# Block-sparse attention with a gated feed-forward: three split products for half of chunk 0's down-projection, and a later start of chunk 1's attention

## The chip, the cores and the metric

One core of a Trainium2 chip runs the whole program. The metric is the device time in microseconds (us), the median of several runs. The engines are TensorE (PE in the profile; PEld is its weight load), VectorE (DVE), ScalarE (ACT), GpSimd (POOL) and SyncE (SP). SyncE and GpSimd serve here mainly as queues that issue DMAs.

## The reference

```python
mask = |blk_i - blk_j| <= 1  or  an edge block (0 or 23) in row or column
mask |= the 3 sampled key blocks of the query's block
attn = softmax(where(mask, q @ k.T / 8, -1e9))       # 4 batches, 8 heads, 768 x 64, blocks of 32
x = (attn @ v) as [3072 tokens, 512]
h = x @ w_in                                          # 512 -> 2048
out = (h * sigmoid(1.702 * h)) @ w_out                # 2048 -> 512
```

Everything is float32. The two weight matrices reach the kernel as 64-bit words and are turned into float32 on the chip.

## The kernel before

**Chunks and steps.** The 3072 tokens are cut into 6 chunks of 512. A chunk's feed-forward is 16 steps, one for each block f of 128 of the 2048 inner columns. Step m (`tick`, L644) has f = m mod 16. In it TensorE makes 12 products for the up-projection of block f (`up`, L492: four slices of 128 inputs, three products each), and then the down-projection of the step before (`down`, L534), which adds to four PSUM banks. ScalarE and VectorE make the gate between them (`gate`, L506): a tanh from PSUM, and g = (tanh + 1) * h. In steps 0 to 12 ScalarE first copies h out of its one PSUM bank (L514), so the next step's up-projection can have that bank once the copy is done.

**Split products.** TensorE takes float32 operands either plainly (one product is then two instructions) or in a reduced form, `float32r`, one instruction. A value is split into a high part (a cast by ScalarE) and a low part (value minus high part, by VectorE); high x high, high x low and low x high add up to the product. Every up-projection does that. The down-projection does it from chunk 1 on: L562 and L563 take ghi with the two parts of the weight, L558 takes glo with the high part. `gate_hi` (L519) casts g to ghi behind the first half of the down-projection, `gate_lo` (L526) makes glo at the start of the next step, and the weight's parts lie in a ring of three tiles `wout`, which `split` (L486) fills from `wst`, read back from DRAM (`stream`, L480). In chunk 0 the down-projection is plain: four products a step, two in each half (L546), from g and the float32 weight `whole[f]`.

**Unpacking the weights.** During chunk 0 the generator `weights` (L407) turns the 64-bit words into float32, block by block, in the order w_in 0, w_in 1, w_out 0, w_in 2, w_out 1, and so on. For each block GpSimd's queue fetches 512 KB (L426, five blocks ahead); ScalarE makes a first pass over the high words into a tile `a` (L438); VectorE does three integer operations on it (L449, L456, L463). For w_in, ScalarE then casts the high part (L467) and VectorE makes the low part while the next block is under way (L453). `a` is one of two tiles in rotation. For w_out the first pass writes a tile of the `ghi` or `glo` ring instead, where the finished weight stays as `whole[f]`, and SyncE's queue copies it to DRAM (L470, `ws`), from where chunks 1 to 5 read it. The first pass over w_out block f waits in the generator until at most four blocks are ahead of the down-projection (L459). Each `yield` ends a piece; a step runs 8 pieces if an attention unit begins in it, else 9: none or two at its start, four between tanh and g, four or three at its end (L649).

**The attention.** A chunk's tokens are 8 units. Chunk 0's attention runs before step 0; chunk 1's is put between the steps of chunk 0 by `plan` (L605), in quarters of a step: a unit's scores at its starting quarter, its transposes four quarters later, and its values where the next unit's scores stand. The 8 units share quarters 4 to 56 evenly (starts 4, 10, 17, 23, 30, 36, 43, 49). Behind each starting quarter `loads` (L223) issues the keys that a freed buffer can take: on SyncE's queue four transfers and six more whose address comes from a register, each waiting until TensorE is through with the buffer.

**Order.** The program order is written out by hand; each engine and each queue works through its own instructions strictly in it, and waits where a tile is not ready or not yet free.

Of the kernel before, what the change touches and what calls it, by code (L numbers as in the profile page):

```python
# [9 lines left out]
F32 = mybir.dt.float32  # L10
F32R = mybir.dt.float32r
I32 = mybir.dt.int32
AF = mybir.ActivationFunctionType
ALU = mybir.AluOpType
# [4 lines left out]
P = 128  # L19
# [5 lines left out]
DM = H * D  # L25
DF = 2048
NCT = DM // P
NF = DF // P
# [7 lines left out]
WRING = 3  # L36
LAG = 1
QT = 4
BIG = float(2 ** 33)
SCALE = 1.0 / float(D) ** 0.5  # L40
REBASE = 2.0 ** -112
AHEAD = 5


class Kernel:
# [361 lines left out]
    def weights(self):  # L407

        nc = self.nc
        todo = []  # L410
        for f in range(NF + LAG):
            if f < NF:
                todo.append((f, 0))
            if f >= LAG:
                todo.append((f - LAG, 1))
        self.ready = set()
        tiles = {}

        def fetch(k):
            if k < len(todo):  # L420
                f, i = todo[k]
                if i == 0:
                    raw = self.const.tile([P, 2 * DM], I32, name=f"win{f}")
                else:
                    raw = self.work.tile([P, 2 * DM], I32, name="raw", bufs=3)
                nc.gpsimd.dma_start(out=raw, in_=self.w64[i][f])  # L426
                tiles[k] = {"raw": raw.rearrange("p (a b) -> p a b", b=2)}

        def first(k):


            f, i = todo[k]
            if i == 0:
                a = self.work.tile([P, DM], I32, name="a")
            else:
                a = self.work.tile([P, DM], F32R, name=("ghi", "glo")[f % 2]).bitcast(I32)
            tiles[k]["a"] = a
            nc.scalar.activation(out=a.bitcast(F32), in_=tiles[k]["raw"][:, :, 1].bitcast(F32), func=AF.Abs, scale=REBASE)  # L438

        for k in range(AHEAD):  # L440
            fetch(k)
        yield
        first(0)
        yield
        for k, (f, i) in enumerate(todo):
            fetch(k + AHEAD)
            raw, a = tiles[k]["raw"], tiles[k]["a"]
            low, high = raw[:, :, 0], raw[:, :, 1]
            nc.vector.tensor_scalar(out=a, in0=a, scalar1=3, scalar2=None, op0=ALU.logical_shift_left)  # L449
            yield  # L450
            if k > 0 and todo[k - 1][1] == 0:
                t, w = self.win[todo[k - 1][0]], tiles[k - 1]["a"].bitcast(F32)
                nc.vector.tensor_tensor(out=t[:, DM:2 * DM], in0=w, in1=t[:, 0:DM].bitcast(F32), op=ALU.subtract)  # L453
                self.ready.add(todo[k - 1])
                yield
            nc.vector.scalar_tensor_tensor(out=a, in0=high, scalar=-0x80000000, in1=a, op0=ALU.bitwise_and,  # L456
                                           op1=ALU.bitwise_or)
            if k + 1 < len(todo):
                while todo[k + 1][1] == 1 and (not self.turned or todo[k + 1][0] - 4 > self.downs - 1):  # L459
                    yield  # L460
                first(k + 1)
            yield
            nc.vector.scalar_tensor_tensor(out=a, in0=low, scalar=29, in1=a, op0=ALU.logical_shift_right,  # L463
                                           op1=ALU.bitwise_or)
            if i == 0:
                self.win[f] = self.const.tile([P, 2 * DM], F32R, name=f"win{f}")
                nc.scalar.copy(out=self.win[f][:, 0:DM], in_=a.bitcast(F32))  # L467
            else:
                self.whole[f] = a.bitcast(F32)
                nc.sync.dma_start(out=self.ws[f], in_=self.whole[f])  # L470
                self.ready.add((f, i))
            yield

    def need(self, f, i):
        while (f, i) not in self.ready:
            next(self.conv, None)
# [40 lines left out]
        self.g[m] = [g]  # L517

    def gate_hi(self, m):  # L519
        if m < NF:  # L520
            return
        ghi = self.work.tile([P, CT], F32R, name="ghi")
        self.nc.scalar.copy(out=ghi, in_=self.g[m][0])  # L523
        self.g[m].append(ghi)
# [9 lines left out]
    def down(self, m, part):  # L534
        nc = self.nc
        if m < 0:
            return
        c, f = divmod(m, NF)
        if c == 0:
            self.need(f, 1)  # L540
        o = [self.bank[3 + n] for n in range(NN)]
        tk = [slice(n * P, (n + 1) * P) for n in range(NN)]
        last = f == NF - 1
        if c == 0:
            for n in range(2 * part, 2 * part + 2):
                nc.tensor.matmul(o[n], self.g[m][0][:, tk[n]], self.whole[f], start=(f == 0), stop=last)  # L546
            if part == 1:
                del self.g[m]
                self.downs = m + 1
                if last:  # L550
                    self.store(c, o)
            return
        _, ghi, glo = self.g[m]
        w = self.wout[m % WRING]
        woh, wol = w[:, 0:DM], w[:, DM:2 * DM]

        def low(n):
            nc.tensor.matmul(o[n], glo[:, tk[n]], woh, start=False, stop=last)  # L558

        if part == 0:  # L560
            for n in self.order(c):
                nc.tensor.matmul(o[n], ghi[:, tk[n]], woh, start=(f == 0), stop=False)  # L562
                nc.tensor.matmul(o[n], ghi[:, tk[n]], wol, start=False, stop=False)  # L563
                if last:
                    low(n)
            return
        if not last:
            for n in range(NN):
                low(n)
        del self.g[m]  # L570
        self.downs = m + 1
        if last:
            self.store(c, o)
# [31 lines left out]
    def plan(self):  # L605

        chunks = [[g for g in self.items if g["unit"]["n"] // CU == c] for c in range(NC)]
        at, starts = {}, []
        for c in range(1, NC):
            begin = 4 if c == 1 else 4 * QT * (4 * c - 4) - 8  # L610
            end = 4 * QT * 4 * c - 8
            dense = sum(not self.sparse(g) for g in chunks[c])
            room, count = end - begin - 4 * dense, len(chunks[c]) - dense
            for k, g in enumerate(chunks[c]):
                q = room + 4 * (k - count)
                if self.sparse(g):
                    q = min(8 * k, room - 6 * (count - k)) if room >= 7 * count else room * k // count
                starts.append((begin + q, g))
        starts.append((end, None))
        put = lambda q, part, g: at.setdefault(q, []).append((part, g))  # L620
        for k, (q, g) in enumerate(starts):
            before = starts[k - 1][1] if k else None
            turn = q + 4
            if g is not None:
                if q >= 0:
                    put(q, self.scores, g)
                turn = q + (4 if self.sparse(g) else 2)
                put(turn, self.transposes, g)
            if before is not None:
                assert q >= 0  # L630
                put(q, self.values, before)
                if before["end"]:
                    put(turn, self.turn, before)
        return at
# [49 lines left out]
    def first(self):  # L684
# [19 lines left out]
        for p in range(CU // 2):  # L704
# [20 lines left out]
            if final:  # L725
                weights(1)
            finish(behind)
            behind = self.transposes(b)
            if final:
                self.turned = True  # L730
                weights(2)
            finish(behind)
            if final:
                weights(1)
# [76 lines left out]
```

## Time and profile before

| | |
|---|---|
| median of 3 runs | 782.81 us (782.76 to 785.66) |
| profiled execution | 784.16 us, span 782.5 us |
| TensorE busy | 749.5 us (96% of the span) |
| VectorE busy | 395.5 us (51%) |
| ScalarE busy | 364.8 us (47%) |
| chain of waits | TensorE 92%, DMA 5% |

The span is what the trace covers; the profiled execution's own time is 1.7 us longer. A busy TensorE is one whose matmul records leave no gap. The shares are averages: chunk 0, from about 61 to 204 us, has other proportions than the rest, since the weights are unpacked there. In the timelines below a duration is that of one instruction; instructions of one engine overlap a little, so the time that one costs its engine is the distance between two starts.

### The profile page before, as it was taken

The numbers are of one execution on the slowest core, as the hardware profiler recorded it, in microseconds if no ns is written. First come the engines' busy times: TensorE is split into PE (matmuls) and PEld (weight loads), VectorE is DVE, ScalarE is ACT, GpSimd is POOL, SyncE is SP. The second block draws the span as 40 slices with busy tenths as digits, with TensorE's granted clock in tenths as the row PEclk, the third lists the DMA queues.
The fourth block names the chain that finished last, engine by engine and source line by source line (L and its number), as shares of the span: only waits on it lengthen the run. The fifth ranks groups of instructions, "written<-read, shape, count | busy, mean of one in ns | idle before, by whom it ended". The sixth has DMA issues, their size and how long they took to land.

```text
span 782.5 us, 19089 instructions
## 1 busy us (share of the span) xinstructions
PE 749.5 (96%) x7520; PEld 559.9 (72%) x7520; DVE 395.5 (51%) x1044; ACT 364.8 (47%) x919; POOL 68.4 (9%) x109
## 2 busy tenths in 40 slices
PE   3778999999999999999999999999999999999997
PEld 2554666666777777777777777777777777888885
DVE  4367888863554354445445544444554444443333
ACT  3374575643555444444444544444545444333232
POOL 3342122100000001000000000000000000000000
PEclk9899999999999999999999999999999999999999
DMA  8989988764744437564444455435574231141111
GB/s 247 326 295 345 314 286 310 239 203 142 219 146 144 125 107 226 164 175 136 150 122 141 144 175 147 145 116 154 162 234 156 82 108 29 40 107 42 54 41 54
DMA packets 62235, 128.20 MB, mean 164 GB/s; under 512 B 7713, under 2 KB 27938, under 8 KB 61634
## 3 DMA queue, kind: packets, MB, share of 16 engines
q1 hardware_dynamic: 49954, 85.09, 36.0%
q0 software_dynamic: 11376, 41.03, 15.6%
q8 instruction: 59, 0.97, 0.5%
q10 hardware_dynamic: 816, 0.86, 0.4%
q14 instruction: 30, 0.25, 0.1%
HBM read 116.47 MB, written 10.49 MB: 162 GB/s over the span
## 4 chain that ended last, share of the span: by engine, by line
PE 92%; DMA 5%; SPq 1%; issue 1%; DVE 0%; POOL 0%; ACT 0%; POOLq 0%; DVEq 0%
PE bank L501 13%; PE bank L503 11%; PE bank L502 11%; PE bank L562 10%; PE bank L558 10%; PE bank L563 10%; PE bank L546 7%; PE bank L314 6%; PE bank L340 5%; PE bank L263 5%; DMA kg<-in_kb_dram 2%; PE bank L348 2%; PE bank L275 2%; DMA vmid<-in_v_dram 1%; PE bank L393 1%; DMA vown<-in_v_dram,vidx 1%
## 5 line engine op out<-in xcount | busy, mean ns | idle before, releaser
L501 PE MATMUL bank<-xhi,win 128*128 128x512 f32 x384 | 164.4, 428 | 0.6 <-ACT xhi L400 0.5
L516 DVE SCALAR_TENSOR_TENSOR g<-g,bank 128x512 f32<-128x512 f32 x83 | 57.0, 687 | 190.8 <-ACT g L509 190.8
L503 PE MATMUL bank<-xhi,win 128*128 128x512 f32 x384 | 152.1, 396 | 0.4 <-DVE win L453 0.4
L502 PE MATMUL bank<-xlo,win 128*128 128x512 f32 x384 | 151.9, 396 | 0.0
L298 ACT ACTIVATE ex<-bank,nm 128x256 f32<-128x256 f32 (+1 forms) x176 | 84.7, 491 | 130.0 <-DVE nm L286 130.0
L509 ACT ACTIVATE g<-bank 128x512 f32<-128x512 f32 x96 | 57.5, 598 | 158.9 <-PE bank L503 158.9
L562 PE MATMUL bank<-wout,ghi 128*128 128x512 f32 x320 | 128.6, 402 | 0.0
L563 PE MATMUL bank<-wout,ghi 128*128 128x512 f32 x320 | 126.3, 395 | 0.0
L490 DVE TENSOR_TENSOR wout<-wst,wout 128x512 fp32r<-128x512 f32 x80 | 55.4, 692 | 78.3 <-ACT wout L489 77.3
L558 PE MATMUL bank<-wout,glo 128*128 128x512 f32 x320 | 90.1, 395 | 0.0
L501 PEld LDWEIGHTS bank<-xhi,win 128*128 128x128 f32 x384 | 72.5, 189 | 21.6 <-issue 2.7
L286 DVE CUSTOM_DVE_ANT_1 bank<-bank,bias 128x256 f32<-128x256 f32 x176 | 73.7, 441 | 24.8 <-PE bank L263 20.3
L503 PEld LDWEIGHTS bank<-xhi,win 128*128 128x128 f32 x384 | 72.4, 189 | 18.7 <-DVE win L453 0.7
L502 PEld LDWEIGHTS bank<-xlo,win 128*128 128x128 f32 x384 | 72.6, 189 | 16.5 <-issue 2.6
L219 POOL DMA_INDIRECT vown<-in_v_dram,vidx x44 | 43.1, 980 | 409.9 <-PE bank L340 292.5
L523 ACT CAST ghi<-g 128x512 fp32r<-128x512 f32 x80 | 49.7, 621 | 45.5 <-DVE g L516 45.5
L558 PEld LDWEIGHTS bank<-wout,glo 128*128 128x128 f32 x320 | 60.1, 188 | 14.7
L319 ACT COPY pt<-bank 128x512 f32<-128x512 f32 (+1 forms) x112 | 56.9, 560 | 29.0 <-PE bank L314 28.9
L562 PEld LDWEIGHTS bank<-wout,ghi 128*128 128x128 f32 x320 | 60.2, 188 | 13.8
L563 PEld LDWEIGHTS bank<-wout,ghi 128*128 128x128 f32 x320 | 60.2, 188 | 13.5
L263 PE MATMUL bank<-kg,qt 64*32 64x256 f32 x1408 | 52.0, 399 | 15.3 <-DMA kg<-in_kb_dram 13.2
L531 DVE TENSOR_TENSOR glo<-g,ghi 128x512 fp32r<-128x512 f32 x80 | 54.7, 684 | 0.7 <-ACT ghi L523 0.7
(101 smaller groups left out, 890.1 us busy)
## 6 DMA issues: line engine op xcount, KB each, us to landing
wst<-ws SPq DMA_DIRECT2D x80, 256.0 KB
kg<-in_kb_dram SPq DMA_DIRECT2D x142, 128.0 KB
kg<-in_kb_dram SPq DMA_DIRECT2D x22, 384.0 KB
win<-in_moe_w_in_dram POOLq DMA_DIRECT2D x16, 512.0 KB, 8.3
raw<-in_moe_w_out_dram POOLq DMA_DIRECT2D x16, 512.0 KB, 4.3
kg<-in_kT_dram SPq DMA_DIRECT2D x4, 1536.0 KB
vown<-in_vd_dram SPq DMA_DIRECT2D x8, 768.0 KB
qt<-in_q_dram SPq DMA_DIRECT2D x22, 256.0 KB
```

The source lines that it names most:

```text
L263: nc.tensor.matmul(sps[h][BLK * c:BLK * (c + 1), n * i:n * (i + 1)].rearrange("p (n s) -> p n s", s=BLK), self.qt[r][rows, bi, UT * pair + ...
L286: nc.vector.tensor_tensor_reduce(out=at, in0=at, in1=bias, scale=-SCALE, scalar=3.0e38, op0=ALU.add, op1=ALU.min, accum_out=un["nm"][:, ha ...
L298: nc.scalar.activation(out=ex, in_=sps[h][:, n * k:n * (k + 1)], func=AF.Exp, bias=un["nm"][:, half, c:c + 1], scale=-1.0, accum_out=un["r ...
L319: copies.append(lambda pt=pt, ps=ps, m=m: nc.scalar.copy(out=pt[:, 0:m], in_=ps[:, 0:m]))
L501: nc.tensor.matmul(h, wih[:, k], hi[:, k], start=(k == 0), stop=False)
L502: nc.tensor.matmul(h, wih[:, k], lo[:, k], start=False, stop=False)
L503: nc.tensor.matmul(h, wil[:, k], hi[:, k], start=False, stop=(k == NCT - 1))
L509: nc.scalar.activation(out=g, in_=self.h, func=AF.Tanh, scale=0.851)
L516: nc.vector.scalar_tensor_tensor(out=g, in0=g, scalar=1.0, in1=h, op0=ALU.add, op1=ALU.mult)
L558: nc.tensor.matmul(o[n], glo[:, tk[n]], woh, start=False, stop=last)
L562: nc.tensor.matmul(o[n], ghi[:, tk[n]], woh, start=(f == 0), stop=False)
L563: nc.tensor.matmul(o[n], ghi[:, tk[n]], wol, start=False, stop=False)
```

## The change

In chunk 0 the down-projection of blocks 8 to 15 takes the split form of the later chunks; blocks 0 to 7 stay plain. For it the unpacked w_out block f (f of 8 and more) lies in a tile `a`, is copied to DRAM from there, and is split at once into the ring `wout` (ScalarE's cast, and VectorE's low part in `rest`). The first pass over such a block waits until at most three blocks are ahead (the length of that ring). `gate_hi` and `gate_lo` work from step 8 on. Chunk 1's units share quarters 8 to 56 instead of 4 to 56 (starts 8, 14, 20, 26, 32, 38, 44, 50). Chunk 0's sums are stored by the code that the later chunks use.

```diff
+NFULL = 8
...
-            if i == 0:
+            if i == 0 or f >= NFULL:
                 a = self.work.tile([P, DM], I32, name="a")
             else:
                 a = self.work.tile([P, DM], F32R, name=("ghi", "glo")[f % 2]).bitcast(I32)
...
+        def rest(k):
+            t, w = tiles[k]["to"], tiles[k]["a"].bitcast(F32)
+            nc.vector.tensor_tensor(out=t[:, DM:2 * DM], in0=w, in1=t[:, 0:DM].bitcast(F32), op=ALU.subtract)
+            self.ready.add(todo[k])
...
-            if k > 0 and todo[k - 1][1] == 0:
-                t, w = self.win[todo[k - 1][0]], tiles[k - 1]["a"].bitcast(F32)
-                nc.vector.tensor_tensor(out=t[:, DM:2 * DM], in0=w, in1=t[:, 0:DM].bitcast(F32), op=ALU.subtract)
-                self.ready.add(todo[k - 1])
+            if k > 0 and "to" in tiles[k - 1]:
+                rest(k - 1)
                 yield
...
-                while todo[k + 1][1] == 1 and (not self.turned or todo[k + 1][0] - 4 > self.downs - 1):
+                while todo[k + 1][1] == 1 and (not self.turned or todo[k + 1][0] - (4 if todo[k + 1][0] < NFULL else WRING) > self.downs - 1):
                     yield
                 first(k + 1)
...
             if i == 0:
-                self.win[f] = self.const.tile([P, 2 * DM], F32R, name=f"win{f}")
-                nc.scalar.copy(out=self.win[f][:, 0:DM], in_=a.bitcast(F32))
+                self.win[f] = tiles[k]["to"] = self.const.tile([P, 2 * DM], F32R, name=f"win{f}")
+            elif f >= NFULL:
+                nc.sync.dma_start(out=self.ws[f], in_=a.bitcast(F32))
+                tiles[k]["to"] = self.wout[f % WRING]
+            if "to" in tiles[k]:
+                nc.scalar.copy(out=tiles[k]["to"][:, 0:DM], in_=a.bitcast(F32))
             else:
...
+        rest(len(todo) - 1)
+        yield
...
     def gate_hi(self, m):
-        if m < NF:
+        if m < NFULL:
             return
...
-        if c == 0:
+        if m < NFULL:
             for n in range(2 * part, 2 * part + 2):
                 nc.tensor.matmul(o[n], self.g[m][0][:, tk[n]], self.whole[f], start=(f == 0), stop=last)
             if part == 1:
                 del self.g[m]
                 self.downs = m + 1
-                if last:
-                    self.store(c, o)
             return
...
-            begin = 4 if c == 1 else 4 * QT * (4 * c - 4) - 8
+            begin = 8 if c == 1 else 4 * QT * (4 * c - 4) - 8
```

## Rows read from the trace of the kernel before

**Rows 1.** The page's chain that ended last, shares by engine.

```profile
PE 92%; DMA 5%; SPq 1%; issue 1%; DVE 0%; POOL 0%; ACT 0%; POOLq 0%; DVEq 0%
```

**Rows 2.** Stretches: length, busy time of each engine, PEclk, DMA share, GB/s.

```profile
60.00:78.00 18.00, 14.68 (x76) 8.85 (x77) 14.19 (x31) 8.40 (x20) 4.15 (x6) 0.91 0.97 341
78.00:130.00 52.00, 52.00 (x545) 33.02 (x544) 43.52 (x106) 31.99 (x78) 11.94 (x18) 1.00 0.91 302
130.00:160.00 30.00, 30.00 (x293) 18.85 (x291) 25.52 (x61) 18.89 (x45) 5.83 (x8) 1.00 0.79 259
```

**Rows 3.** The chain in order of time, 60 to 260 us: start, duration, what.

```profile
70.19 0.43 PE bank L502
...
73.58 3.43 PE bank L546 x8
...
77.02 0.87 PE bank L314 x8
...
80.70 1.02 PE bank L263 x32
...
81.73 1.03 PE bank L340 x64
...
176.13 1.02 PE bank L263 x32
...
209.53 0.93 PE bank L558 x4
```

**Rows 4.** TensorE's timeline, end of step 0 and step 1: start, duration, instruction.

```profile
64.58 0.39 PE L503 MATMUL bank<-xhi,win 128*128 128x512 f32 x1
66.99 0.62 PE L263 MATMUL bank<-kg,qt 64*32 64x256 f32 x4 [2.02 <-DMA vmid<-in_v_dram]
67.94 1.53 PE L263 MATMUL bank<-kg,qt 64*32 64x256 f32 x28 [0.33 <-DMA kg<-in_kb_dram]
```

**Rows 5.** ScalarE's timeline in step 0.

```profile
65.50 0.58 ACT L514 COPY wst<-bank 128x512 f32<-128x512 f32 x1
65.97 0.68 ACT L438 ACTIVATE a<-win 128x512 f32<-128x512 f32 x1
```

**Rows 6.** SyncE's queue, a load of keys and the copy behind it.

```profile
137.19 0.38 SPq L190 DMA_DIRECT2D qt<-in_q_dram  x1
...
145.76 0.44 SPq L470 DMA_DIRECT2D ws<-glo  x1
```

**Rows 7.** VectorE's timeline in steps 10 and 11.

```profile
150.79 0.43 DVE L286 CUSTOM_DVE_ANT_1 bank<-bank,bias 128x256 f32<-128x256 f32 x1
...
152.56 0.14 DVE L286 DVE_READ_ACCUMULATOR2_ANT nm<- 128x1 f32 x1
152.90 0.68 DVE L463 SCALAR_TENSOR_TENSOR ghi<-raw,ghi 128x512 int32<-128x512 int32 x1
153.50 0.42 DVE L449 TENSOR_SCALAR a<-a 128x512 int32<-128x512 int32 x1
153.95 0.69 DVE L456 SCALAR_TENSOR_TENSOR a<-win,a 128x512 int32<-128x512 int32 x1
154.68 0.69 DVE L463 SCALAR_TENSOR_TENSOR a<-win,a 128x512 int32<-128x512 int32 x1
...
159.39 0.68 DVE L516 SCALAR_TENSOR_TENSOR g<-g,wst 128x512 f32<-128x512 f32 x1
159.99 0.16 DVE L369 TENSOR_SCALAR rg<-rs 128x4 f32<-128x4 f32 x1
...
160.59 0.68 DVE L463 SCALAR_TENSOR_TENSOR a<-win,a 128x512 int32<-128x512 int32 x1
```

**Rows 8.** Groups by line and shape: busy, mean ns, idle before, releaser.

```profile
L453 DVE TENSOR_TENSOR win<-a,win 128x512 fp32r<-128x512 f32 x16 | 11.1, 691 | 6.6 <-ACT win L467 6.5
```

**Rows 9.** The page's DMA issues: count, KB each, median us to landing.

```profile
win<-in_moe_w_in_dram POOLq DMA_DIRECT2D x16, 512.0 KB, 8.3
raw<-in_moe_w_out_dram POOLq DMA_DIRECT2D x16, 512.0 KB, 4.3
```

## The prediction

> **What bounds the kernel now.** I read the page first: TensorE holds 92% of the chain of waits that ended last [rows 1]. So the reader should see that a microsecond is won only by issuing less on TensorE or by closing one of its few gaps, and lost wherever another engine makes it wait. Second, the table of stretches [rows 2]: inside the part that the change touches (steps 0 to 15, about 61 to 204 us) TensorE has no idle time after 78 us, its clock is full from there (2.4 GHz), and VectorE is the next engine, busy for 43.5 of 52 us and then for 25.5 of 30 us until the weights are unpacked. The DMA engines are 0.97 and 0.91 busy early, 0.79 by 130 to 160 us. So TensorE is the bound, with VectorE a tenth to a sixth behind it, and the early stretch has one gap. Third, the timelines of the engines, for what stands in whose queue.
>
> **The products.** A plain float32 product of 128x512 is issued as two instructions; eight of them advance the chain by 3.43 us, so one product costs 0.857 us. Four split products advance it by 0.93 us, 0.233 each, three of them 0.70 [rows 3]. Eight steps with four products each: 32 x (0.857 - 0.70) = 5.1 us less, all of it on the bound: **-5.1**. The weight loads lie under the products already.
>
> **The moved start.** In step 1 TensorE issues its last product of step 0 at 64.58, then waits 2.02 us and 0.33 us for the first unit's loads; behind it the clock falls (28 score products take 1.53 us where 32 take 1.02, and the next six products come 0.43 apart) [rows 3, 4]. Up to the transposes at 77.02 that is 12.2 us after the product that ends near 64.8, for 1.02 + 12 x 0.233 + 3.43 = 7.25 us of work at full clock. With the unit a step later, step 1's up-projection goes next. What is late then is its single PSUM bank: ScalarE reads step 0's sums until 65.50 + 0.58 = 66.1 [rows 5], 1.3 us of waiting. The scores come at about 72 us; in the trace their data was there at 67.9. Gain 12.2 - 7.25 - 1.3 = 3.7: **-3.7**. If the clock falls all the same, the gain is 1.8 less (0.6 on the scores, six products at 0.43 instead of 0.233), so 1.9; without the bank's wait 5.0. The loads that the units' scores trigger move with them, from steps 2, 5, 9 and 12 to 3, 6, 9 and 12; units now start every 6 quarters. The load of the first moved unit was issued before step 0 and stays.
>
> **Edits at nothing.** ScalarE gets a cast of g and a cast of the weight in each of eight steps, 0.62 us each; it is busy for 18.9 of 30 us in 130 to 160 us [rows 2], which hides them unless it stands still (below). The sums of chunk 0 are stored from the end of step 16 as before. The DMA bytes are the same.
>
> **The new wait.** From weight block 8 on, the unpacked down-projection weight lies in tile *a*, of which there are two, instead of *ghi/glo*. Its copy to DRAM is issued by SyncE, and ScalarE's first pass over block f+1 (L438) writes the same *a*, so it must wait until the copy of block f has landed. By the generator's yields the copy of block 10 is asked for in step 9 and the pass over block 11 stands at that step's end. Between them, in SyncE's order, stands a load of keys: its first transfer waits for the scores of the unit in quarter 38. One such load holds the queue from 137.19 to 145.76, 8.6 us, with a copy issued only behind it [rows 6]. Queued behind the waiting ScalarE pass are the cast of win, the copies of transposed weights and the next tanh; on VectorE L449 waits for the pass, and behind L449 stands the split of g (L531), which TensorE needs at the end of the next down-projection.
>
> The copy's landing has no row. The nearest are the weight fetches of 512 KB from the same engines: median 4.3 us and 8.3 us [rows 9]; half of 4.3 for half the bytes, 2.2 us, is my lower end, 8.3 the upper. I take 4.3, since the copy and that fetch are issued at the same point of the program. From the end of the scores: 8.6 + 4.3 + 0.6 (the pass, 0.68 busy, where the next instruction starts before its end [rows 5]) + 0.45 (L449) + 0.60 (the split) = 14.5 us until g's low part is there. TensorE meanwhile has values 1.03, down 12 x 0.233, up 2.8, eight transposes 0.87 and two turns at the same rate 0.22, and the eight high products 1.87: 9.6 us. It waits 4.9 us in step 10: **+4.9** (2.8 at a landing of 2.2, 8.9 at 8.3).
>
> The Trainium skill ("DMA: Bandwidth & Descriptors", section "Anatomy of one DMA — SWDGE (gpsimd) path") gives a DMA 2.0 us plus its bytes over 436 KB per us, mostly the receipt of the write. By that 256 KB land in an estimated 2.6 us and this wait would be 3.2 us instead of 4.9; no row here shows a copy landing on this queue.
>
> **VectorE behind it.** Its work per step, by starts of successive instructions [rows 7]: unpacking two blocks 2 x (0.45 + 0.73 + 0.60) and two low parts at 0.60 = 4.8; g 0.60; the split 0.60: 6.0. A unit adds 1.77 (four minima), 0.34, and 0.60 for factors and the low part of x: 2.7, twice in three steps. Three steps: 18.0 + 5.4 = 23.4 us. TensorE's step was (176.13 - 77.02)/12 = 8.26 [rows 3]; less 0.64, and with units every 6 instead of 6.5 quarters 0.17 more, 7.8: three steps 23.4. So in steps 10 to 13 VectorE has no slack, and each further wait at L449 comes through. Between a copy's request and the next L449, VectorE has 3.0 to 3.6 us of its own work, while copy and pass take 4.9 to 5.0: 1.4 and 2.0 us of waiting. In step 12 the second key load again holds the copy: scores end about 2 us before VectorE's list of that step begins, which lasts 8.0; the pass is done 8.6 + 4.3 + 0.6 = 13.5 after the scores: about 3.2 more. Sum **+6.6**. At a landing of 2.2 only 1.1 of it is left, and then the low parts wait for their casts as one does now (0.41 us each, six of them, from the 6.6 us before 16 such instructions [rows 8]): 3.6. After step 14 the unpacking ends and VectorE's load falls; the delay stays.
>
> **The clock.** The waits of 2.02 and 0.33 us were followed by products at 1.2 GHz up to about 72 us [rows 3, 4], worth 1.8 us. Of the waits above at least one is longer; where VectorE is late anyway a slow TensorE costs nothing. I charge it once: **+1.8** (0 to 3.6).
>
> **Sum.** -5.1 - 3.7 + 4.9 + 6.6 + 1.8 = +4.5 us. The profiled execution took 784.16 us for a span of 782.5, 1.35 over the median of 782.81; I carry the difference to the median: **787.3 us**. This case by itself spans 783 to 792 (landings of 3.3 to 5.3 us).
>
> **Rivals.**
> *Short landing.* If copies land in 2.2 us: -8.8 + 2.8 + 3.6 = -2.4, 780.4 us. (The Trainium skill's 2.6 us, from the page above, comes close to it.) For it: a copy is half a fetch, and the DMA engines are down to 0.79 busy by then. Against: beside it runs a fetch of 512 KB, and keys stand ahead in the same queue.
> *The wait never reaches TensorE* (the other side). If SyncE issues the copy before the load's transfers, or the pass finds its tile free, only VectorE's cast waits are left: -8.8 + 2.5 = -6.3, 776.5 us. It decides at 9.6 us after the scores: a split that starts earlier costs nothing. For it: before the change TensorE never idles from 78 to 160 us [rows 2] though VectorE is so full. Against: rows 6 show exactly this copy behind this load.
> *Long landing.* At 6.3 us: 6.9 + 12.6 + 1.8 - 8.8 = +12.5, 795.3 us. For it: the fetches of win take 8.3 at 0.91 busy. Against: the later waits fall where the DMA load is lower.
>
> **Numbers.** Forecast 0.55, short landing 0.20, no wait 0.13, long landing 0.12. About 0.5% (3.9 us) is what a measurement can tell from no change: 778.9 to 786.7 counts as the same. The forecast's case splits 0.33 slower, 0.22 same; short landing 0.17 same, 0.03 faster; no wait 0.12 faster, 0.01 same; long landing all slower. Faster 0.15, same 0.40, slower 0.45. Range 776.5 to 795: from the no-wait case to the long landing, with the far tails left out.
>
> **What would show it.** Right: four split products in 0.93 us at L546's old place; scores of the first moved unit near 72 us with no wait for DMA; a copy of *ws* from *a* some 8.6 us after the scores of quarter 38; ScalarE idle before L438 until a DMA on *ws*; TensorE idle before L558 until L531 in step 10 and again in step 13; a stretch at 1.2 GHz after one of them. Wrong: L438 never waits for *ws*, or TensorE is without gaps to 200 us; then the no-wait sum holds. A chunk 0 that ends later than 210 us by more than 12 us would mean longer landings, or a VectorE chain that I priced too short.

## The result and the profile after

| | before | after |
|---|---|---|
| median, 6 runs each | 783.88 us (782.76 to 785.66) | 794.03 us (792.33 to 795.93) |
| ratio | | 1.0129, 95% interval 1.011 to 1.0148 |
| profiled execution (span) | 784.16 (782.5) | 792.33 (790.3) |

The change makes the kernel slower by 10.1 us in the medians and by 7.8 us between the two profiled spans. The forecast was +4.5 us: the sign was right, the size less than half of what the medians show. The profiled execution of after is the fastest of its six; the other five have spans of 791.2 to 793.9 and mean granted clocks of 0.973 to 0.979 against its 0.984. The rest of this section accounts for its 7.8 us.

The chain that ended last on the page of after (TensorE's share in [rows 1] was 92%):

```profile
PE 77%; SPq 2%; DVE 1%; issue 1%; DMA 1%; ACT 1%; ACTq 0%; DVEq 0%
```

Two stretches of after, columns as in [rows 2], and behind them the second one as it was before:

```profile
130.00:160.00 30.00, 23.52 (x264) 16.96 (x263) 20.96 (x50) 16.55 (x36) 2.71 (x5) 0.83 0.51 170
160.00:204.00 44.00, 41.05 (x445) 31.33 (x444) 29.71 (x75) 25.10 (x65) 4.80 (x5) 0.96 0.53 170
...
160.00:204.00 44.00, 44.00 (x517) 27.73 (x516) 20.60 (x65) 19.08 (x55) 3.76 (x4) 1.00 0.53 165
```

In 130 to 160 us TensorE was without a gap before; now it is idle for 6.5 us there and for 2.9 us in 160 to 204, and the granted clock falls to 0.83 and 0.96. VectorE is less busy in 130 to 160 than it was (21.0 against 25.5 us): it stands still too.

**The moved start.** TensorE's timeline at step 1 of after (start, duration, instruction, idle before):

```profile
64.64 0.39 PE L513 MATMUL bank<-xhi,win 128*128 128x512 f32 x1
66.19 0.50 PE L511 MATMUL bank<-xhi,win 128*128 128x512 f32 x1 [1.16 <-ACT wst L524]
...
72.63 1.09 PE L264 MATMUL bank<-kg,qt 64*32 64x256 f32 x32
```

There is no DMA wait and no slow clock ([rows 4] had both); instead 1.16 us for the bank of h. The scores end at 73.7 where the same work, scores, up- and down-projection, was done at 77.02 before: 3.3 us gained.

**The products.** The eight high and four low products of one step of after, from the first of them to the transposes behind (start, duration, instruction):

```profile
162.46 0.39 PE L570 MATMUL bank<-wout,ghi 128*128 128x512 f32 x1
...
165.25 1.04 PE L315 MATMUL bank<-ident,ex 128*128 128x128 f32 x8
```

**The held copy.** SyncE's queue in steps 9 to 12 of after; the answer to [rows 6]:

```profile
137.36 0.34 SPq L191 DMA_DIRECT2D qt<-in_q_dram  x1
...
146.14 7.18 SPq L472 DMA_DIRECT2D ws<-a  x2
...
170.47 0.34 SPq L191 DMA_DIRECT2D qt<-in_q_dram  x1
...
178.82 0.37 SPq L472 DMA_DIRECT2D ws<-a  x1
```

The load of keys begins with the end of the scores and the copy from *a* (blocks 10 and 13) is issued 8.8 and 8.4 us later. What the copies' line says of who waited, and how long the copies took to land (min, median, max):

```profile
  ACT a L439: 16.2, 3
...
DMA to landing us min/median/max: 2.0/2.3/3.2
```

The last line rests on only three of the eight copies, for the trace assigns a landing to no more. The third wait, the first in time, is for the copy of block 8 (SyncE's, ScalarE's and TensorE's timelines):

```profile
119.44 0.39 SPq L472 DMA_DIRECT2D ws<-a  x1
...
125.86 0.67 ACT L439 ACTIVATE a<-raw 128x512 f32<-128x512 f32 x1 [4.80 <-DMA ws<-a]
...
135.67 1.58 PE L264 MATMUL bank<-kg,qt 64*32 64x256 f32 x32 [1.04 <-ACT pt L320]
```

VectorE's last pass over block 8 ended at 118.2, so this copy was held for 1.3 us only; ScalarE's pass could start 6.4 us after its issue, while the DMA engines were 0.87 busy (119.4 to 125.8 us). From 125.86 on either VectorE or ScalarE is at work until the copy of transposed weights at 135.6 that TensorE's scores wait for in step 9: read from the timelines, TensorE's loss there descends from that wait.

The chain of waits of after from the scores ahead of the first held copy, that of block 10, to the point where TensorE goes on (start, duration, what):

```profile
135.67 1.68 PE bank L264 x32
...
146.14 3.08 DMA ws<-a
149.32 0.67 ACT a L439
150.01 0.43 DVE a L455
150.44 0.12 DVE glo L541
...
150.96 0.70 DVE win L443
151.68 0.68 ACT a L439
152.36 0.48 ACT g L519
152.84 0.47 ACT wst L524
153.32 0.53 ACT wout L475
...
154.47 0.69 DVE a L460
155.16 0.61 DVE g L526
...
156.32 0.38 ACT xhi L401
156.72 0.44 DVE xlo L402
157.20 1.93 PE bank L341 x64
```

It leaves TensorE at the scores, runs through SyncE's queue and the copy's landing (3.08 us), and comes back not at g's low part (L541, 150.4) but at the values (L341) at 157.20. Between them stand, in order: the low part of win, the next pass, tanh, the copy of h, a cast, another integer pass, g, and the two parts of x. TensorE's own timeline at both places:

```profile
146.64 0.40 PE L571 MATMUL bank<-wout,ghi 128*128 128x512 f32 x1
151.09 1.22 PE L566 MATMUL bank<-wout,glo 128*128 128x512 f32 x2 [4.05 <-DVE glo L541]
...
154.37 2.65 PE L264 MATMUL bank<-kg,qt 64*32 64x256 f32 x32 [1.20 <-ACT pt L320]
157.20 0.31 PE L341 MATMUL bank<-vown,pt 128*32 128x64 f32 x1 [0.18 <-DVE xlo L402]
...
179.73 0.39 PE L571 MATMUL bank<-wout,ghi 128*128 128x512 f32 x1
182.96 1.19 PE L566 MATMUL bank<-wout,glo 128*128 128x512 f32 x4 [2.84 <-DVE glo L541]
186.15 0.32 PE L341 MATMUL bank<-vown,pt 128*32 128x64 f32 x1
```

From the end of the high products (146.9) to the values it has 0.93 + 1.02 = 1.95 us of work at full clock (four low products and the scores) and takes 10.3: 8.4 us lost. At the second place, from 180.0 to 186.15, 4.2 us. At both places the scores, slowed by the clock, end only 0.1 to 0.2 us before the values start (157.02 and 186.05), so this trace alone can't tell which of the two limits, the slow clock or the parts of x, sets the loss; the zeros below can. What the clock did there:

```profile
151.00:154.00 3.00, 2.07 (x4) 1.16 (x4) 2.41 (x6) 2.32 (x5) 0.49 (x1) 0.50 0.06 22
154.00:160.00 6.00, 5.45 (x98) 3.96 (x99) 5.26 (x15) 3.18 (x7) 0.04 (x1) 0.50 0.38 123
183.00:188.00 5.00, 4.89 (x101) 3.06 (x102) 4.30 (x11) 2.91 (x6) 0.00 (x0) 0.66 0.10 36
```

### The profile page after: what moved, and what is told of

It is laid out like the page before. It is cut to its first block, busy times and chain, and to the rows that moved or that the text cites. A ratio compares the mean times of both kernels' runs of the same rounds, so it can differ in the third digit from the quotient of the medians.

```text
span 790.3 us, 19186 instructions
## 1 busy us (share of the span) xinstructions
PE 747.1 (95%) x7552; PEld 568.2 (72%) x7552; DVE 404.9 (51%) x1060; ACT 374.2 (47%) x935; POOL 67.9 (9%) x109
## 4 chain that ended last, share of the span: by engine, by line
PE 77%; SPq 2%; DVE 1%; issue 1%; DMA 1%; ACT 1%; ACTq 0%; DVEq 0%
PE bank L511 11%; PE bank L570 10%; PE bank L566 10%; PE bank L513 10%; PE bank L571 10%; PE bank L512 10%; PE bank L315 4%; PE bank L341 4%; PE bank L264 4%; PE bank L349 2%; PE bank L276 2%; PE bank L394 1%; SPq L202 1%; DMA ws<-a 1%; SPq L201 1%
## 5 line engine op out<-in xcount | busy, mean ns | idle before, releaser
L511 PE MATMUL bank<-xhi,win 128*128 128x512 f32 x384 | 160.6, 418 | 1.8 <-ACT wst L524 1.2
L513 PE MATMUL bank<-xhi,win 128*128 128x512 f32 x384 | 151.9, 396 | 0.4 <-DVE win L443 0.4
L570 PE MATMUL bank<-wout,ghi 128*128 128x512 f32 x352 | 141.7, 403 | 0.0
L571 PE MATMUL bank<-wout,ghi 128*128 128x512 f32 x352 | 138.9, 395 | 0.0
L566 PE MATMUL bank<-wout,glo 128*128 128x512 f32 x352 | 100.4, 399 | 6.9 <-DVE glo L541 6.9
L566 PEld LDWEIGHTS bank<-wout,glo 128*128 128x128 f32 x352 | 66.4, 189 | 23.8 <-DVE glo L541 7.8
L533 ACT CAST ghi<-g 128x512 fp32r<-128x512 f32 x88 | 54.6, 621 | 50.7 <-DVE g L526 50.7
L570 PEld LDWEIGHTS bank<-wout,ghi 128*128 128x128 f32 x352 | 66.2, 188 | 15.3
L571 PEld LDWEIGHTS bank<-wout,ghi 128*128 128x128 f32 x352 | 66.2, 188 | 14.8
L541 DVE TENSOR_TENSOR glo<-g,ghi 128x512 fp32r<-128x512 f32 x88 | 60.2, 684 | 1.4 <-ACT ghi L533 1.4
```

Source lines behind the costliest of these rows:

```text
L511: nc.tensor.matmul(h, wih[:, k], hi[:, k], start=(k == 0), stop=False)
L513: nc.tensor.matmul(h, wil[:, k], hi[:, k], start=False, stop=(k == NCT - 1))
L541: self.nc.vector.tensor_tensor(out=glo, in0=g, in1=ghi.bitcast(F32), op=ALU.subtract)
```

## The experiments

Each kernel was measured together with the kernel before (783.94, 784.99 and 784.12 us in three groups), and its ratio is to that time. Theory Q: the copy is held on SyncE's queue behind a key load and the pass over the next block waits for it. Rivals: VectorE has no room (V), the slow clock is the larger part (C, later K). Names in code type are those used further down.

**Another queue for the copy (`copy_on_scalar`).**

```diff
-                nc.sync.dma_start(out=self.ws[f], in_=a.bitcast(F32))
+                nc.scalar.dma_start(out=self.ws[f], in_=a.bitcast(F32))
```

> The copies of blocks 8 to 15 are issued on ScalarE's queue instead of SyncE's, so no key load stands ahead of them. Theory Q (the copy held behind a key load on SyncE's queue is the loss): ScalarE's waits for ws (16.2 us in 3 in the changed kernel) fall below 2 us, TensorE has no gap over 1 us from 78 to 204 us, and the kernel takes 775 to 778 us, under both. Rival V (VectorE has no room for two more passes a step, the copy only shows where it was late anyway): still 786 us or more. Rival C (slow clock after any short wait): between, 781 to 786.

Measured: 782.66 us, ratio 0.9972 (0.9945 to 0.9999). Its waits from 60 to 212 us (total, times, longest):

```profile
ACT a L439 <- DMA ws<-a: 6.1, 5, 2.1
...
PE bank L264 <- ACT pt L320: 1.8, 1, 1.8
...
PE bank L341 <- DVE xlo L402: 1.0, 1, 1.0
```

The longest wait for a copy falls from 6.2 to 2.1 us and about 12 us of time come back (0.9972 against 1.0129), so V is out as the main cause. It misses the 775 to 778 expected of Q, and the waits for copies are 6.1 us in all where less than 2 was expected: five waits for a landing remain, 0.7 to 2.1 us each, and at one place TensorE waits 1.8 and 1.0 us with 6.8 us of slow clock. The time lies in the range given for rival C, and C fits what is left here: 2.8 us of waits and at most 3.4 us of stretched products, against 8.4 of gains, leave about the 2.2 us that the ratio shows. No run takes that rest apart.

**The order on the same queue (`load_later`).**

```diff
+    def begin(self, q, load=True):
...
-        self.loads()
+        if load:
+            self.loads()
...
-        after = self.begin(QT * m + 2)
+        after = self.begin(QT * m + 2, m >= NF)
         if moe:
             self.gate(m, lambda: run(n1))
+        self.loads()
```

> The change, with the key loads of a step's third quarter issued behind the pieces between tanh and g, so that the copy stands ahead of the load on SyncE's queue. Two tiles a as before. Theory Q: the copy is issued as soon as it is asked for and the pass waits only for its landing, as with the copy on ScalarE's queue: waits for ws of 2 us at most, 780 to 784 us. If the hold was something else than the order on the queue, 790 us or more.

Measured: 782.15 us, ratio 0.9978 (0.9959 to 0.9997), within the expected time. No work was changed, only the place in program order where a step's third quarter issues its loads (keys, and values where a buffer is free), and 12 us come back against the change. ScalarE's wait for copies:

```profile
ACT a L439 <- DMA ws<-a: 6.6, 3, 2.7
```

The hold is gone, the landing is still waited for, up to 2.7 us where 2 at most had been expected. The two kernels agree: the hold costs about 12 us, and waits for a landing are part of what is left.

**A third tile (`three_a`).**

```diff
-                a = self.work.tile([P, DM], I32, name="a")
+                a = self.work.tile([P, DM], I32, name="a", bufs=3)
```

> Three tiles a instead of two; copies stay on SyncE's queue. Theory Q: the pass over w_out block 11 no longer waits, but that over w_in block 13, which now gets block 10's tile, still waits for the same copy one third of a step later, so a rest of 1 to 2 us at each of the two loads stays: 777 to 781 us. Rival V: 786 us or more, as before. A result of 790 or more would speak against Q.

Measured: 778.86 us, ratio 0.9945 (0.992 to 0.9969): under both kernels, inside the range for Q, but without the rest of 1 to 2 us that Q expected at each load. The copies are held as before, for the key load of step 9 takes SyncE's queue from 135.12 to 143.65, but no wait for *ws* is left. Its stretch:

```profile
130.00:160.00 30.00, 28.96 (x355) 22.39 (x357) 26.40 (x64) 21.85 (x52) 4.08 (x6) 1.00 0.68 222
```

VectorE is busy for 26.4 of 30 us and TensorE idle for 1.04 us only, a wait of the values for a part of x. The profiled span is 775.1 us, 7.4 under before's 782.5: the 8.4 us of the two gains (5.1 and 3.3) less that gap. So two more passes a step fit into VectorE; rival V is refuted for the split from block 8.

**The zeros in the wait (`fill_the_wait`).**

```diff
+        if part == 1 and m in FILL:          # FILL = {9: 17, 12: 12}, self.none is a tile of zeros
+            for k in range(FILL[m]):
+                nc.tensor.matmul(o[k % NN], ghi[:, tk[k % NN]], self.none, start=False, stop=False)
```

> The change, with products by a tile of zeros put between the high and the low products in step 10 (17 of them, 4 us) and step 13 (12, 2.8 us), where TensorE waits for g's low part; the sums are not changed. They keep TensorE busy through the wait. Theory K (the slow clock behind the waits, 10.2 and 3.4 us in the trace, is the largest part of the loss): the time falls by about 5 us, to 788 to 790 us. Theory W (what is queued on ScalarE and VectorE behind the held pass sets when TensorE may go on to the values, and the slow clock before that point is hidden): the fall is only what lies after that point, (160.2 - 157.2)/2 + (187.5 - 186.2)/2 = 2.2 us, 791 to 793 us.

Measured: 792.87 us, ratio 1.0121 (1.0089 to 1.0153), no difference from the change that can be measured. Stretches, the chain at the first place, and the start of the values at both:

```profile
130.00:160.00 30.00, 27.66 (x290) 20.76 (x289) 22.14 (x54) 17.02 (x42) 2.43 (x5) 0.94 0.52 177
160.00:204.00 44.00, 41.05 (x457) 31.98 (x456) 27.61 (x71) 24.03 (x60) 4.94 (x5) 1.00 0.54 171
```

```profile
133.81 1.67 PE bank L267 x32
...
154.62 0.31 PE L344 MATMUL bank<-vown,pt 128*32 128x64 f32 x1 [0.34 <-DVE xlo L405]
...
184.89 0.24 PE L344 MATMUL bank<-vown,pt 128*32 128x64 f32 x1 [0.96 <-DVE xlo L405]
```

The clock of 130 to 160 us is 0.94 instead of 0.83 and that of 160 to 204 is 1.00 instead of 0.96, yet the time stays: the values of the first place start at 154.62, 19 us after the scores of step 9 ended (135.5), where it was 20 us in the change, and at both places TensorE still waits for the part of x (0.34 and 0.96 us), at the second with its clock at 1.00. (The key load of the second place took 10.0 us here against 8.4, so the times there can't be compared.) K's 5 us, a ratio of 1.0065, lie outside the interval, so K falls. W fits; its 2.2 us can't be told from nothing. The slow products lay for the most part inside a wait that ScalarE and VectorE end.

**The two parts alone (`start_only`, `split_only`).**

```diff
-            begin = 4 if c == 1 else 4 * QT * (4 * c - 4) - 8      # start_only: in the kernel before
+            begin = 8 if c == 1 else 4 * QT * (4 * c - 4) - 8
...
-            begin = 8 if c == 1 else 4 * QT * (4 * c - 4) - 8      # split_only: in the changed kernel
+            begin = 4 if c == 1 else 4 * QT * (4 * c - 4) - 8
```

> The kernel before with chunk 1's units from quarter 8 and nothing else. Every theory: the gap of 2.35 us and the slow clock behind it in step 1 go, 1.2 us of waiting for the bank of h comes: 3.3 us less (2 to 4), 780 to 782 us. If it is slower than before, the moved key loads cost something by themselves.

Measured: 781.97 us, ratio 0.9971 (0.9949 to 0.9992): faster by 2.3 us by the ratio (2.0 by the medians), at the lower end of 2 to 4. TensorE's waits in its step 0 and 1 (the first was 0.43 us before):

```profile
63.29 0.39 PE L503 MATMUL bank<-xhi,win 128*128 128x512 f32 x1 [0.86 <-DVE win L453]
...
66.95 0.50 PE L501 MATMUL bank<-xhi,win 128*128 128x512 f32 x1 [1.17 <-ACT wst L514]
```

> The change with the units from quarter 4 as before. Key loads then fall in steps 2, 5, 9 and 12, that of step 9 at its start, so the copy of block 10 is asked for after most of it. Theory Q: the hold in step 9 is shorter by about half a step, the kernel takes 3.3 us more for the start and 4 to 8 less at that place: 786 to 793 us. Rival V: 3.3 us more than the change, 797 us.

Measured: 791.51 us, ratio 1.0086 (1.0053 to 1.0118): slower than before without any moved start, and within the range for Q, outside that for V. The waits for copies are 10.3 us against 16.2 in all. The longest, for the copy of block 10:

```profile
148.39 10.83 SPq L472 DMA_DIRECT2D ws<-a  x2
...
154.08 0.66 ACT L439 ACTIVATE a<-raw 128x512 f32<-128x512 f32 x1 [5.72 <-DMA ws<-a]
```

VectorE's last pass over block 10 ended at 146.2, so the copy is held for 2.2 us here, against 7.4 in the change (138.8 to 146.14): shorter by half a step and more, as Q had it. But the 5.7 us of waiting are nearly all landing, and a landing of that length was no part of Q's estimate, so that the time fits Q is partly luck.

**How early the split may begin, with three tiles.** NFULL = 4, 6 and 10 instead of 8, and three tiles together with the later load.

> Three tiles a, and the split form from block 4 on instead of 8: four more steps with 0.64 us less on TensorE, 2.5 us in all, for two more VectorE passes in each. If VectorE has room in steps 4 to 7 (it is busy 43.9 of 52 us there with three tiles): 776 to 777 us. If it is full there: 779 us or more, with TensorE waiting for g's low part in these steps.

Measured: 784.74 us, ratio 1.0008 (0.9988 to 1.0028). Its stretches:

```profile
100.00:130.00 30.00, 25.86 (x280) 19.69 (x282) 25.03 (x59) 18.45 (x44) 6.02 (x9) 0.90 0.77 255
130.00:160.00 30.00, 27.38 (x305) 21.08 (x298) 23.96 (x60) 18.81 (x44) 6.07 (x9) 0.92 0.69 230
```

TensorE idles 4.1 and 2.6 us, before scores that wait for copies of transposed weights on ScalarE; it does not wait for g's low part, as the expectation had it. The chain of waits behind the longest of them, from 96.3 to 125.9 us, holds nothing but VectorE's and ScalarE's instructions and 12% for handing over between them (no gap over 0.6 us), while VectorE alone is busy for 24.5 of those 29.6 us. So it is the two engines in turn, not VectorE alone, that have no room for the split there.

> Three tiles a, split form from block 6. From block 4 TensorE waited 3.6 and 2.6 us for copies of transposed weights in steps 6 to 10 and lost what the products gave. If VectorE's room runs out gradually: 1.3 us less products against one wait of 1 to 2 us, the same as from block 8 within 1 us, 778 to 780 us (with the kernel before at 784). If it is the length of the stretch with 8 pieces a step that counts, 781 us or more.

Measured: 778.24 us, ratio 0.9927 (0.9905 to 0.9949), the same as from block 8.

> Three tiles a, split form from block 10: 1.3 us more on TensorE than from block 8, and VectorE has two steps fewer at their fullest. If the 1.04 us gap of the version from block 8 (values waiting for the low part of x) and what else VectorE's fullness costs goes: 778 to 779 us, no difference. If nothing else was lost there: 780 us.

Measured: 778.48 us, ratio 0.9923 (0.9893 to 0.9953).

> Three tiles a and the key loads of a step's third quarter behind its unpacking pieces, together. Theory Q has nothing left to hold after either: the same as three tiles alone, 777 to 779 us. If a remainder of the hold is still in three tiles alone, 1 to 2 us less.

Measured: 778.4 us, ratio 0.992 (0.989 to 0.9951). From block 6, 8 or 10 and with or without the later load, three tiles give 778.2 to 778.9, some 0.5 to 0.8% under the kernel before; the runs don't order these four.

## Why the prediction was right and wrong

**What bounds.** Right. TensorE alone decides, and the new wait reaches it. (By the rows quoted, VectorE is about a sixth short of full in both stretches.)

**The products.** Right: eight high products and four low ones take 2.8 us in the trace of after (162.46 to 165.25) where eight plain instructions took 3.43, so 5.1 us in eight steps.

**The moved start.** Right in its mechanism, 3.3 us in the trace of after against 3.7; alone it was worth 2.0 to 2.3 us.

**The hold on SyncE's queue.** Right: 8.8 us measured against 8.6 at the copy of block 10, and 8.4 at that of block 13. `load_later` shows it by itself.

**The landing.** I took 4.3 us for all. It took 3.1 and 2.3 us at the two held copies, and about 6.4 at that of block 8, which I had not priced. For the two, the estimate of 2.6 us from the Trainium skill ("DMA: Bandwidth & Descriptors", "Anatomy of one DMA — SWDGE (gpsimd) path") was nearer than my row of a fetch; the page gives its figure for GpSimd's path, and these copies are issued by SyncE. With the 3.1 us of block 10 the prediction's sum gives a wait of 3.7 us before the low products (L566 after the change); 4.05 was measured, where I had 4.9.

**The failing step** is "The new wait", in its sentence "It waits 4.9 us in step 10". The sum ended at the first thing that TensorE needs behind the held pass, g's low part. Two pieces later TensorE needs the next unit's values, and these wait for the two parts of x, which stand 6.8 us of ScalarE's and VectorE's queues behind the release (150.4 to 157.2). The text names what is queued behind the pass and then prices only the split. So the two held copies cost 8.4 + 4.2 = 12.6 us where 4.9 + 3.2 = 8.1 had been put. A smaller omission: I looked for a wait at blocks 10 and 13 only, and the copy of block 8, hardly held but slow to land, cost 1.5 us in step 9.

**VectorE behind it.** Wrong as a mechanism. "VectorE has no slack" in steps 10 to 13 is refuted by `three_a`, and the 1.4 and 2.0 us of waiting for copies without a load ahead did not show: ScalarE waits for the copies of blocks 8, 10 and 13 only, and TensorE has no gap between 160 and 180 us. (With the split from block 4 VectorE and ScalarE in turn do lack room, as `NFULL` = 4 above showed.)

**The clock.** I charged 1.8 us. The slow stretches were longer than I had thought: 7.5 us of busy time at half clock in 151 to 160, so half of it lost, and a third of 4.9 us lost in 183 to 188, together 5.4 us. But only what lay behind the values could count, (160.2 - 157.2)/2 + (187.5 - 186.2)/2 = 2.2 us, and `fill_the_wait` shows that removing most of the slow stretch gives nothing measurable.

**The sum as measured.** Gains 3.3 + 5.1; losses 12.6 at the two places, 2.2 of slow clock behind them, 1.5 in step 9 (1.04 idle before scores that then took 1.58 instead of 1.09): 16.3 - 8.4 = 7.9 against 7.8 of the spans. Two errors of the forecast cancelled in part, and that is luck: the 3.4 us charged for waits of copies without a load ahead did not come, and covered most of the 4.5 us missing at the two held copies; without them the forecast would have been +1.1 us. The medians differ by 2.3 us more; the five other runs' lower clocks (0.973 to 0.979) lie beside it, and this part stays open.

**The rivals.** *Short landing* had the right landing and the wrong time, because it shared the failing step. *The wait never reaches TensorE* describes `three_a`: it measured 778.9 where the case gave 776.5. The 6.3 us of *Long landing* were met once, at the copy of block 8 with the DMA engines 0.87 busy, and not at the held copies.

## What to carry to other kernels

When a DMA out of a rotating tile is added, ask what stands ahead of it on its queue in program order before asking how long it takes: here another issue order gave back 12 us, and one more tile, which also hides the landing, 14. When an in-order engine is made to wait, follow its queue past the first consumer to each result that the bound engine needs in the next step, and price the last of them. A bound engine that idles and then runs at the slow clock has one loss, not two, as long as another engine still ends the wait, as ScalarE and VectorE did here.

## What the runs showed of the hardware that I had not expected

The slow stretch lasted while TensorE was busy again: at clock 0.50 (1.2 GHz) in all of 154 to 160 us, with 5.45 of 6.00 us busy. With products by zeros in the wait the clock of 130 to 160 us rose from 0.83 to 0.94. A copy of 256 KB from SBUF to DRAM landed in 2.0 to 3.2 us where the trace has its landing (three copies in 160 to 204 us, the DMA engines 0.53 busy in that stretch), and one issued with them 0.87 busy kept its tile for 6.4 us; fetches of twice the size took 4.3 and 8.3 us in the median [rows 9].
